# Linear attention into a routed feed-forward layer: every expert run twice, its first 256 rows after 16 routed tiles, the rest at the end

## The chip, the cores and the metric

One core of a Trainium2 chip. TensorE (PE) multiplies, VectorE (DVE), ScalarE (ACT) and GpSimd (POOL) work on tiles in SBUF and PSUM, SyncE (SP) issues transfers. The metric is the device time of one execution in microseconds; less is better. Inputs and outputs are in HBM, in 32-bit floats.

## The reference

```python
# attention: q, k, v of shape (8 batches, 8 heads, 576, 64)
kv  = einsum('bhsd,bhse->bhde', k, v)
out = einsum('bhsd,bhde->bhse', q, kv)
out = out / sqrt(mean(out*out, -1) + 1e-6) * g_norm
x   = out, heads side by side          # 4608 tokens x 512
# routed layer: 8 experts, each token goes to one
e_idx  = argmax(x @ w_gate)            # 512 x 8
gate_w = softmax(x @ w_gate)[e_idx]
eom    = sigmoid(x @ w_output_gate)
for e in range(8):
    rows = (e_idx == e)
    y[rows] = gate_w * eom[:, e] * (relu(x[rows] @ w1[e]) @ w2[e])   # 512 -> 1024 -> 512
```

How many tokens an expert gets is known only after the routing. The kernel gives the experts, sorted by their number of rows, fixed capacities (`CAP`: 704, 704, 640, 620, 600, 576, 576, 576 rows); what does not fit goes through an overflow loop at the end, which runs as often as a register says.

## The kernel before

Tokens are worked in 36 tiles of 128. **Attention**: `kv_part(b)` multiplies keys by values for one batch (4.5 tiles), `kvT_part` and `m_part` fold the gate weights in, and `out_tile(g)` multiplies a tile's queries by the result, so that one product gives the attention rows and the parts of the router's logits by head. ScalarE copies the rows (`xrow`), their squares (`sq`) and the logit parts (`gp`) out of PSUM; VectorE sums the squares (`sums`). Rows go to a table `xs` in HBM (`xwrite`).

**Routing** runs for a group of tiles at a time (`GR`: 10, 10, 4 and 12 tiles). `route(gi)` is a generator of some 40 small VectorE steps, with two groups of matmuls on TensorE (`rps`, which counts a token's place within its expert, and `tblps`, which sums the table of row numbers) and one-hot tiles `la` made mostly on GpSimd. `advance()` moves each routing to its next pause; where it is called is written out by hand (`WAITS`, `HOOKS`, `TAIL`).

**Experts**: a run of an expert takes up to 704 rows. `gather` fetches rows from `xs` by an indirect transfer on GpSimd's queue, `scale_rows` multiplies by the norm, `stage` transposes a tile on TensorE, and copies it as `xT`. For precision each operand is split into a high and a low part in a reduced format and each product is three matmuls: `split` makes `whi` (ScalarE) and `wlo` (VectorE, sometimes GpSimd) of a weight chunk of 512 KB that `wload` fetched on SP's queue; `mm1(i, f)` is an eighth of the first layer for all rows of run i, followed by the relu and the split of h (`hT`); `mm2(i, k)` is the second layer of one 128-row tile, followed by the scaling (`y`) and the indirect write to `out`. In a run's first layer the second-layer weights are split and the next run's first-layer weights loaded; in its second layer the next run's tiles are staged and its first-layer weights split, and its second-layer weights loaded.

**Order**: after 24 tiles the expert that leads by count so far is found on the chip (`lead_expert`), and its first 384 rows are run (`lead_run`) while the last 12 tiles are being routed. Then the rest of this expert and the seven others follow, in the order of their counts: `RUNS` has nine entries, and each weight is loaded and split once, 64 chunks of each kind. While the third run and the start of the fourth go on, `overflow_list` works out which rows did not fit and writes a small table (`tab`).

Within the blocks `with tc.manual_schedule(engines=...)` each engine works in the order in which the code issues; the engines meet by semaphores. Tiles in SBUF come from 30 slots of 4 KB a partition (`take`, `give`), in turn.

Of the kernel before, what the change touches and what calls it, by code (L numbers as in the profile page):

```python
# [21 lines left out]
P = 128  # L22
# [3 lines left out]
E = 8  # L26
# [10 lines left out]

CAP = [704, 704, 640, 620, 600, 576, 576, 576]  # L40
CMAX = max(CAP)
# [4 lines left out]
GR = (10, 10, 4, 12)  # L46
GROUPS = [list(range(sum(GR[:i]), sum(GR[:i+1]))) for i in range(len(GR))]
GMAX = max(GR)

LEAD_TILES = 24  # L50
LEAD_GROUP = [sum(GR[:i + 1]) for i in range(len(GR))].index(LEAD_TILES)
LEAD = LEAD_TILES * P // E // P * P

RUNS = [(0, 0, LEAD), (0, LEAD // P, CAP[0] - LEAD)] + [(p, 0, CAP[p]) for p in range(1, E)]


XD = min(4, 1024 // LEAD)
HF = 1024 // (2 * LEAD)

SLOTS = 30  # L60

SPARE = 3
# [3 lines left out]
BIG = {26: 5, 31: 5}  # L66

HOOKS = {15: 'R', 27: 'RR', 28: 'R', 31: 'RGW', 32: 'X', 34: 'NL'}
TAIL = "QLLLLRRRSLSRRSLLRRRLSLRRSRLSLL"

WAITS = {(0, 2): 3, (1, 7): 2, (1, 2): 0, (1, 8): 2, (1, 5): 0, (0, 8): 2, (0, 6): 2}

GPSIMD_GROUPS = 1
APART = (2,)


SPLITS = ['VV', 'AV', 'AV', 'AV', 'AP', 'AP', 'AP', 'AP']  # L80
NORMS = ("PPP", "VPVP")
PLACES = ['P', 'P', 'PAV', 'PAV', 'PAV']
# [14 lines left out]
K_I = K_C + E * TMAX  # L97
# [3 lines left out]
def constants():  # L101
# [13 lines left out]
    k[:, K_C:K_C + E * TMAX] = ((e[:, None] * NT + np.arange(TMAX)) * P).reshape(-1)  # L115
    k[:, K_I:K_I + P] = m
# [14 lines left out]
MAN = {ET.PE, ET.Activation, ET.DVE, ET.Pool}  # L131
# [3 lines left out]
def body(ctx: ExitStack, tc: tile.TileContext, kvm, rem, qT, wg, gn, w1, w2, kc, xs, tab, out):  # L135
# [3 lines left out]
    cst = ctx.enter_context(tc.tile_pool(name="cst", bufs=1))  # L139
    cf = cst.tile([P, K_N], F32, name="cf")  # L140
# [14 lines left out]
    gidx = cst.tile([P, E, TMAX], I32, name="gidx")  # L155
    oidx = cst.tile([P, E, TMAX], I32, name="oidx")
# [6 lines left out]
    ps_b = main.enter_context(tc.tile_pool(name="ps_b", bufs=2, space=psum))  # L163
    ps_t = main.enter_context(tc.tile_pool(name="ps_t", bufs=2, space=psum))
    ps_y = main.enter_context(tc.tile_pool(name="ps_y", bufs=1, space=psum))
    free = list(range(SLOTS))
    held = {}

    def take(shape, dt, name):

        i = free.pop(0)
        t = mem.tile(shape, dt, name=name, tag=f"slot{i}")
        held[id(t)] = (i, t)
        return t

    def give(t):
        free.append(held.pop(id(t))[0])
# [12 lines left out]
    def wload(p, which, c, eng=None):  # L190
        r = take([P, 1024], F32, "wraw")
        eng = eng or nc.sync
        src = (w1 if which == 1 else w2)[ds(expert(p, eng), 1), c]
        d = eng.dma_start(out=r, in_=src.rearrange("o p x -> p (o x)"))
        raw[(p, which, c)] = r
        return d

    def split(p, which, c, eng=None):
        r = raw.pop((p, which, c))
# [34 lines left out]
    def gather(i):  # L234
        p = RUNS[i][0]
        rows = xs[0:1 + LEAD_TILES * P] if i == 0 else xs
        for t, c0, M in tiles_of(i):
            x = take([P, XW], F32, "xg")
            nc.gpsimd.indirect_dma_start(  # L239
                out=x[:M, :], out_offset=None, in_=rows,  # L240
                in_offset=bass.IndirectOffsetOnAxis(ap=gidx[:M, p, t:t + 1], axis=0))
            xg[(p, t)] = x
# [6 lines left out]
    def scale_rows(i):  # L249
        for k, (t, c0, M) in enumerate(tiles_of(i)):  # L250
            if i < 2 and NORMS[i][k] == "V":
                continue
            scale_heads(xg[(RUNS[i][0], t)][:M], nc.gpsimd)

    def stage(i, k):
        p = RUNS[i][0]
        t, c0, M = tiles_of(i)[k]
        x = xg.pop((p, t))
        if i < 2 and NORMS[i][k] == "V":
            scale_heads(x[:M], nc.vector)  # L260
        if k == 0:
            if i == 0:
                xT[i] = [[take([P, XD, LEAD], F32R, "xT") for _ in range(4 // XD)] for _ in range(2)]
            else:
                xT[i] = [[mem.tile([P, 4, CMAX], F32R, name="xT", tag=f"xT{j}")] for j in range(2)]
        tl = cst.tile([P, 1], F32, name="tl", bufs=14)
        nc.vector.tensor_copy(tl[:M], x[:M, C_SCALE:C_SCALE + 1])
        tails[(p, t)] = tl
# [4 lines left out]
        for j, (hi, lo) in enumerate(zip(*xT[i])):  # L273
            n = hi.shape[1]
            v = ps[:, j * n:(j + 1) * n, :M]
            nc.scalar.copy(hi[:, :, c0:c0 + M], v)  # L276
            nc.vector.tensor_tensor(out=lo[:, :, c0:c0 + M], in0=v,  # L277
                                    in1=hi.bitcast(F32)[:, :, c0:c0 + M], op=ALU.subtract)
# [5 lines left out]
    def h_of(i, f):  # L284
        return hT[i][f // HF][:, f % HF] if i == 0 else hT[i][:, f]

    def mm1(i, f):
# [3 lines left out]
        J = 1 if C <= 512 else 2  # L291
        N = (C - T) // J
        hi, lo = ([a[:, d] for a in x for d in range(a.shape[1])] for x in xT[i])
        wh, wl = wgt[(1, f // 2)]
        if f == 0:
            if i == 0:
                hT[i] = []
            else:
                hT[i] = hp.tile([P, 8, 2 * CMAX], F32R, name="hT")
        if i == 0 and f % HF == 0:  # L300
            hT[i].append(take([P, HF, 2 * LEAD], F32R, "hT"))
        ps = ps_b.tile([P, 2, 512], F32, name="hps", tag="big")
        for d in range(4):
            o = d * 256 + (f % 2) * P
            for w, x, k in ((wh, hi, 0), (wh, lo, 1), (wl, hi, 2)):
                for j in range(J):
                    n = N + (T if j + 1 == J else 0)
                    nc.tensor.matmul(ps[:, j, :n], w[:, o:o + P], x[d][:, j * N:j * N + n],  # L308
                                     start=(d == 0 and k == 0), stop=(d == 3 and k == 2))
# [863 lines left out]
```

## Time and profile before

| | |
|---|---|
| median of 3 runs | 619.26 us (618.42 to 621.12) |
| the profiled execution | 620.81 us, span 618.8 us |
| TensorE matmul busy | 566.5 us, 92% |
| TensorE weight load busy | 506.3 us, 82% |
| VectorE, ScalarE, GpSimd busy | 263.2, 222.0 and 164.0 us |
| first expert matmul, last expert matmul | at 122.7 us, at 605.7 us |
| read from HBM, written | 72.6 MB, 20.0 MB |
| weight loads | 64 of 512 KB |

The span is counted from the first to the last instruction. A row of the timeline has the start, the duration, the engine, the line of the code and the operands; in brackets stands the idle time in front of it and what ended it. "L308" is the first layer's matmul, "L350" the second's, "L541" a tile's attention, "L474" keys by values, "L317" and "L318" the relu and the split of h, "L214" to "L224" the splits of weights. A matmul in full 32-bit floats (attention) shows as two records.

### The profile page before, as it was taken

The page shows a single profiled execution, that of the slowest core. Times are in us where ns is not written, and L with a number is a line of the kernel's source. Part 1 is how long each engine was busy: PE and PEld are TensorE (multiplying, and loading weights), DVE is VectorE, ACT ScalarE, POOL GpSimd, SP SyncE. Part 2 cuts the span into 40 slices and gives each one's busy share as a digit, 9 for nine tenths or more (in the row PEclk, how much of TensorE's full clock was granted, in tenths as well). Part 3 has the DMA queues.
Part 4 walks back from the last instruction along what each step waited for, and adds up shares of the span by engine and source line. Part 5 has one row for each costly group of instructions (what it writes and reads, how often), then busy time and mean ns, then how long its engine had stood idle before and what let it go on. Part 6 is the DMA issues. An engine that isn't in the chain of part 4 may idle for free.

```text
span 618.8 us, 10459 instructions
## 1 busy us (share of the span) xinstructions
PE 566.5 (92%) x4179; PEld 506.3 (82%) x4179; DVE 263.2 (43%) x536; ACT 222.0 (36%) x413; POOL 164.0 (27%) x163
## 2 busy tenths in 40 slices
PE   3799978848999999999899999999999999999991
PEld 3688868747898998889789988998799889889881
DVE  2123688699425456225331453235135325424300
ACT  1335545634225334323331343234234423523310
POOL 2001044443832510630036117104500630110010
PEclk9958777579999999999999999999999999999996
DMA  8999991770564622349776332524432451110010
GB/s 271 367 409 407 405 366 49 246 285 7 166 231 138 202 89 90 87 169 35 16 159 199 115 122 91 172 69 138 145 112 74 135 181 68 53 52 2 0 47 14
DMA packets 39122, 92.53 MB, mean 150 GB/s; under 512 B 14418, under 2 KB 14546, under 8 KB 39072
## 3 DMA queue, kind: packets, MB, share of 16 engines
q1 hardware_dynamic: 32176, 71.63, 37.4%
q0 software_dynamic: 6464, 20.00, 10.2%
q8 instruction: 34, 0.56, 0.4%
q10 hardware_dynamic: 432, 0.21, 0.1%
q14 instruction: 16, 0.13, 0.1%
HBM read 72.63 MB, written 19.99 MB: 150 GB/s over the span
## 4 chain that ended last, share of the span: by engine, by line
PE 57%; issue 19%; DMA 10%; DVE 4%; POOL 3%; ACT 3%; another core or an unknown queue 2%; SPq 0%; POOLq 0%; DVEq 0%
PE hps L308 24%; PE yps L350 23%; PE ops L541 3%; PE kvps L474 3%; DMA ld<-kvm 3%; DMA xs<-xrow 2%; PE tps L271 2%; POOL out L361 2%; DMA ld<-qT 2%; DMA ld<-rem 2%; PE yps L345 1%; POOL xg L239 1%; DMA wraw<-w 1%; DMA xg<-xs,gidx 1%
## 5 line engine op out<-in xcount | busy, mean ns | idle before, releaser
L308 PE MATMUL hps<-xT,whi 128*128 128x320 f32 (+4 forms) x1024 | 197.3, 310 | 9.5 <-DVE hT L318 8.4
L350 PE MATMUL yps<-whi,hT 128*128 128x512 f32 (+2 forms) x592 | 195.9, 399 | 1.0 <-ACT whi L221 1.0
L308 PEld LDWEIGHTS hps<-xT,whi 128*128 128x128 f32 x1024 | 163.6, 191 | 11.9 <-DVE hT L318 9.1
L350 PEld LDWEIGHTS yps<-whi,hT 128*128 128x128 f32 (+2 forms) x592 | 111.3, 188 | 25.2 <-ACT whi L221 1.2
L308 PE MATMUL hps<-xT,wlo 128*128 128x320 f32 (+4 forms) x512 | 121.6, 309 | 0.0
L318 DVE SCALAR_TENSOR_TENSOR hT<-hps,hT 128x512 fp32r<-128x512 f32 (+5 forms) x112 | 59.2, 529 | 142.6 <-ACT hT L317 142.3
L350 PE MATMUL yps<-wlo,hT 128*128 128x512 f32 (+2 forms) x296 | 116.6, 394 | 0.8 <-DVE wlo L224 0.8
L317 ACT ACTIVATE hT<-hps 128x512 fp32r<-128x512 f32 (+5 forms) x112 | 52.5, 469 | 164.0 <-PE hps L308 121.6
L308 PEld LDWEIGHTS hps<-xT,wlo 128*128 128x128 f32 x512 | 89.0, 191 | 0.0
L361 POOL DMA_INDIRECT out<-y,oidx x42 | 44.8, 1068 | 154.2 <-ACT y L360 107.2
L239 POOL DMA_INDIRECT xg<-xs,gidx x42 | 43.2, 1029 | 137.5 <-PE tps L271 54.6
L350 PEld LDWEIGHTS yps<-wlo,hT 128*128 128x128 f32 (+2 forms) x296 | 55.7, 188 | 12.1 <-DVE wlo L224 1.1
L217 DVE SCALAR_TENSOR_TENSOR wlo<-wraw,gcol,whi 128x1024 fp32r<-128x1024 f32 x32 | 43.9, 1372 | 39.6 <-ACT whi L214 39.6
L247 POOL TENSOR_TENSOR xg<-xg 128x512 f32<-128x512 f32 (+3 forms) x40 | 44.0, 1102 | 43.9 <-DMA xg<-xs,gidx 43.5
L541 PE MATMUL ops<-aug,ld 64*128 64x80 f32 (+1 forms) x640 | 49.0, 327 | 5.8 <-ACT gp L549 5.7
L541 PEld LDWEIGHTS ops<-aug,ld 64*128 64x128 f32 (+1 forms) x640 | 44.5, 230 | 8.8 <-ACT gp L549 6.4
L360 ACT ACTIVATE y<-yps,tl 128x512 f32<-128x512 f32 (+2 forms) x37 | 25.5, 689 | 71.4 <-PE yps L350 68.4
L276 ACT CAST xT<-tps 128x512 fp32r<-128x512 f32 (+3 forms) x45 | 23.6, 530 | 67.6 <-PE tps L271 63.9
L277 DVE TENSOR_TENSOR xT<-tps,xT 128x512 fp32r<-128x512 f32 (+3 forms) x45 | 27.7, 617 | 46.9 <-ACT xT L276 43.3
L474 PE MATMUL kvps<-ld 128*64 128x64 f32 (+1 forms) x640 | 36.4, 300 | 11.1 <-DMA ld<-kvm 10.7
L474 PEld LDWEIGHTS kvps<-ld 128*64 128x64 f32 (+1 forms) x640 | 33.1, 209 | 14.0 <-DMA ld<-kvm 12.0
L224 DVE TENSOR_TENSOR wlo<-wraw,whi 128x1024 fp32r<-128x1024 f32 x28 | 34.3, 1226 | 13.5 <-ACT whi L221 6.7
(158 smaller groups left out, 403.2 us busy)
## 6 DMA issues: line engine op xcount, KB each, us to landing
wraw<-w SPq DMA_DIRECT2D x64, 512.0 KB, 3.2
ld<-kvm SPq DMA_DIRECT2D x32, 512.0 KB, 10.2
ld<-qT SPq DMA_DIRECT2D x18, 512.0 KB, 10.2
xs<-xrow SPq DMA_DIRECT2D x13, 512.0 KB, 10.4
xs<-xrow SPq DMA_DIRECT2D x2, 1280.0 KB, 15.2
ld<-rem SPq DMA_DIRECT2D x3, 512.0 KB, 10.2
xg<-xs,gidx POOLq DMA_INDIRECT x42
out<-y,oidx POOLq DMA_INDIRECT x42
```

What stands on the lines that cost most here:

```text
L217: eng.scalar_tensor_tensor(out=lo, in0=r, scalar=gcol[:, 0:1], in1=hi.bitcast(F32), op0=ALU.mult, op1=ALU.subtract)
L224: eng.tensor_tensor(out=lo, in0=r, in1=hi.bitcast(F32), op=ALU.subtract)
L239: nc.gpsimd.indirect_dma_start(out=x[:M, :], out_offset=None, in_=rows, in_offset=bass.IndirectOffsetOnAxis(ap=gidx[:M, p, t:t + 1], axis=0))
L247: eng.tensor_tensor(out=v, in0=v, in1=f, op=ALU.mult)
L277: nc.vector.tensor_tensor(out=lo[:, :, c0:c0 + M], in0=v, in1=hi.bitcast(F32)[:, :, c0:c0 + M], op=ALU.subtract)
L308: nc.tensor.matmul(ps[:, j, :n], w[:, o:o + P], x[d][:, j * N:j * N + n], start=(d == 0 and k == 0), stop=(d == 3 and k == 2))
L317: nc.scalar.activation(hh, x, AF.Relu)
L318: nc.vector.scalar_tensor_tensor(out=v(h[:, l:l + n]), in0=x, scalar=0.0, in1=hh.bitcast(F32), op0=ALU.max, op1=ALU.subtract)
L350: nc.tensor.matmul(ps[:M], a, b, start=(f == 0 and k == 0), stop=(f == 7 and k == 2))
L361: i_ = nc.gpsimd.indirect_dma_start(out=out, out_offset=bass.IndirectOffsetOnAxis(ap=oidx[:M, p, t:t + 1], axis=0), in_=y[:M], in_offset=N ...
L474: nc.tensor.matmul(ps[u * D:(u + 1) * D, p * D:(p + 1) * D], k, v, start=(s == 0 and p == 0), stop=(s == 4 and p == NP - 1))
L541: nc.tensor.matmul(ps[r0:r0 + m, u, p * W:(p + 1) * W], qt[g // 2][r, p, q0:q0 + m], augs[b % 3][r, p, :], start=True, stop=True)
```

## The change

Every expert runs twice. Its first 256 rows (`ROWS_A`) run in the experts' natural order as soon as the first 16 tiles (`EARLY`) are routed; the rest, 448 to 320 rows of capacity, in the order of counts at the end. `RUNS` has 16 entries, and each weight is loaded and split twice. Where the first 16 tiles hold fewer than 256 rows of an expert, the rows of later tiles still begin at place 256 (`adj`).

The remaining 20 tiles are done by the generator `late()`: key/value products in three pieces, tiles one by one, then the routing's steps up to a pause. A piece follows each eighth of the first layer and each second-layer tile of the first seven runs, ten pieces a run. Their loads go on SP's queue between the weight loads, into eight slots of their own.

```diff
-GR = (10, 10, 4, 12)
+EARLY = 16
+TA = 2
+ROWS_A = TA * P
+GR = (8, 8, 10, 10)
-RUNS = [(0, 0, LEAD), (0, LEAD // P, CAP[0] - LEAD)] + [(p, 0, CAP[p]) for p in range(1, E)]
-SLOTS = 30
+RUNS = [(e, 0, ROWS_A) for e in range(E)] + [(p, TA, CAP[p] - ROWS_A) for p in range(E)]
+SLOTS = 22
+XSLOTS = 8
-GPSIMD_GROUPS = 1
-APART = (2,)
-SPLITS = ['VV', 'AV', 'AV', 'AV', 'AP', 'AP', 'AP', 'AP']
-PLACES = ['P', 'P', 'PAV', 'PAV', 'PAV']
+APART = (1, 2, 3)
+PLACES = ['P', 'PV', 'P', 'P']
+COLD = (2, 20, 8)
-MAN = {ET.PE, ET.Activation, ET.DVE, ET.Pool}
+MAN = {ET.PE, ET.Activation, ET.DVE, ET.Pool, ET.SP}
...
+    def constant(ps, n, start):
+        for _ in range(n):
+            nc.tensor.matmul(ps[0:D, 256:512], ones[:, 0:D], ones.unsqueeze(1).to_broadcast([P, 2, P]), start=start, stop=start)
...   in kv_part, which is now a generator of three pieces
+            if s < 4 and b < FIRST_B:
+                constant(ps, COLD[0] + (COLD[1] if b == 0 and s == 0 else 0), s == 0)
...   in out_tile
+                for c0 in range(r0, r0 + m, D):
+                    q0 = g % 2 * P + c0
+                    for u in range(2):
+                        r = slice(u * D, (u + 1) * D)
+                        nc.tensor.matmul(ps[c0:c0 + D, u, p * W:(p + 1) * W], qt[g // 2][r, p, q0:q0 + D],
+                                         augs[b % 3][r, p, :], start=True, stop=True)
-        nc.scalar.copy(gp[:, t].rearrange("q (p u) x -> q u p x", u=2), v[:, :, :, D:W])
+        nc.scalar.copy(gp[:, t].rearrange("q x (p u) -> q u p x", u=2), v[:, :, :, D:W])
...   at the end of route
+        tps = ps_t.tile([P, 2, E * TMAX], F32, name="tblps", tag="t")
+        for t in range(n):
+            nc.tensor.matmul(tps, las[t], rc[:, t, 0:2], start=(t == 0), stop=(t == n - 1))
+        yield from pause(9)
+        ... tacc gets or adds tps ...
+        if gi == EARLY_GROUP:
+            yield from rows_of_first()
+        if last:
+            yield from rows_of_all()
...
+    def early():
+        ... loads, key/value products of four batches and 16 tiles, with the first expert's first-layer weights behind ...
+        while squares:
+            sums()
+        load(late_loads, xfree, 2)
+        while routing:
+            advance()
+            if routing:
+                constant(ps_t.tile([P, 512], F32, name="cps", tag="t"), COLD[2], True)
+        for c in range(4):
+            wload(0, 2, c)
+        gather(0)
...
+    def run(i, unit):
+        for f in range(8):
+            mm1(i, f)
+            if f % 2:
+                split(i, 2, f // 2)
+                drop(1, f // 2)
+                if not last_run:
+                    wload(i + 1, 1, f // 2)
+            if f == 2 and not last_run:
+                gather(i + 1)
+            if f == 3 and not last_run:
+                scale_rows(i + 1)
+            unit(f)
+        ... staging, splits and loads for the next run between the second layer's tiles, as before ...
+        if i < E:
+            for k in range(T):
+                put(k, 3, unit, 8 + k)
...
+    rest = late()
+        split(0, 1, 0)
+        for k in range(TA):
+            stage(0, k)
+        split(0, 1, 1)
+        for i in range(E - 1):
+            run(i, lambda n: next(rest, None))
+    listing = overflow_list()
+        for i in range(E - 1, len(RUNS)):
+            run(i, lambda n: next(listing, None))
```

All 36 tiles use 64-row blocks of queries now, the splits are all ScalarE's and VectorE's, and the leading run with its search and its hand-written order is gone. In PSUM the late tiles have one pair of banks; the early ones have two.

More of the change, by code (lines that the diff above doesn't have):

```diff
@@ L154, in body @@
     slots = cst.tile([P, NT], F32, name="slots")
-    gidx = cst.tile([P, E, TMAX], I32, name="gidx")
-    oidx = cst.tile([P, E, TMAX], I32, name="oidx")
+    gidx = [cst.tile([P, E, TMAX], I32, name=f"gidx{w}") for w in range(2)]
+    oidx = [cst.tile([P, E, TMAX], I32, name=f"oidx{w}") for w in range(2)]
     novi = cst.tile([P, 1], I32, name="novi")
@@ L290, in mm1 @@
         T = half(i)
-        J = 1 if C <= 512 else 2
-        N = (C - T) // J
-        hi, lo = ([a[:, d] for a in x for d in range(a.shape[1])] for x in xT[i])
+        hi, lo = ([a[:, d] for d in range(4)] for a in xT[i])
         wh, wl = wgt[(1, f // 2)]
         if f == 0:
[L296 to L302, printed above, removed]
+            w = i // E
+            hT[i] = rp_[w].tile([P, 8, 2 * (ROWS_A, CMAX)[w]], F32R, name="hT", tag="hT")
+        ps = ps_h.tile([P, 512], F32, name="hps", tag="h")
         for d in range(4):
@@ L446, in body, with load @@
                 nq += 1
-    def load(spare):
+    late_loads = [l for l in loads if (l[1] >= EARLY // 2 if l[0] is qt else 2 * l[1] >= FIRST_B if l[0] is rt else l[1][0] >= FIRST_B)]
+    loads = [l for l in loads if not any(l is x for x in late_loads)]
+    def load(loads, free, spare=0):
         while loads and len(free) > spare:
@@ L495, in m_part @@
         a = augs[b % 3]
-        ps = ps_b.tile([P, 2, 512], F32, name="mps", tag="big")
+        ps = pair("mps")
         for i in range(2):
@@ L518, in out_tile @@
             gst[gi] = (sm.tile([P, GMAX, E], F32, name="ss"),
[L519 removed]
+                       sm.tile([P, GMAX, 16, H], F32, name="gp"),
                        sm.tile([P, GMAX, 16], F32, name="lg"))
         ss, gp, lg = gst[gi]
[L522 to L525 removed]
+        if not chunk:
+            chunk[:] = [g, take([P, 2, DM], F32, "xrow", xfree)]
         xrow = chunk[1][:, g - chunk[0]]
[L527 removed]
+        ps = pair("ops")
         parts = []
@@ L583, in pause @@
         def pause(k):
-            for _ in range(WAITS.get((gi, k), 1)):
-                yield 1
+            yield 1
         a = sm.tile([P, GMAX, E], F32, name="ra")[:, :n]
@@ L847, in p1_main, with late, more @@
             m_part(b, kvT)
-            while done_tiles < lim:
-                run_out(lim)
-        while done_tiles < NT:
-            run_out(NT)
-        for step in TAIL:
-            act(step)
+            more()
+            while run_out(lim):
+                more()
+        while run_out(EARLY):
+            more()
+        while squares:
+            sums()
+        load(late_loads, xfree, 2)
         while routing:
             advance()
+            if routing:
[3 more added lines that the diff above has]
+        gather(0)
+    def late():
+        def more():
+            load(late_loads, xfree, 1)
+        for b in range(FIRST_B, B + 1):
+            lim = tiles_ready(b - 1)
+            if b < B:
+                kv = kv_part(b)
+                for x in range(3):
+                    cp = next(kv)
+                    more()
+                    yield
+                    if run_out(lim):
+                        more()
+                        yield
+                kvT = kvT_part(cp)
+                yield
+                if run_out(lim):
+                    more()
+                    yield
+                m_part(b, kvT)
+                yield
+            while run_out(lim):
+                more()
+                yield
+        assert not late_loads and done_tiles == NT
+        while squares:
+            sums()
+            yield
+        while routing:
+            advance()
+            yield
     vec = nc.vector
@@ L945, in overflow_list @@
+        yield 1
+        gif = sm.tile([P, E, TMAX], F32, name="gif", bufs=1)
+        vec.tensor_reduce(out=gif[:, :, TA:], in_=t3, axis=AX.X, op=ALU.add)
+        yield 1
+        yield from places(1, gif, TA, TMAX)
     def overflow_list():
```

499 lines of the change are left out of this document (193 added, 306 removed).

## The prediction

> **What bounds the kernel now.** I read the page's slices first, then cut the span where the stages change, because the shares over the whole span mix stages with different limits. The columns are the stretch, its length, the busy time of PE, PEld, DVE, ACT and POOL, the granted clock, the DMA share and GB/s.
>
> ```profile
> core 0: us, PE busy (x) PEld busy (x) DVE busy (x) ACT busy (x) POOL busy (x), PEclk, DMA share, GB/s
> 0.00:34.70 34.70, 21.03 (x324) 17.97 (x324) 5.70 (x15) 7.80 (x19) 3.19 (x7) 0.91 0.95 329
> 34.70:56.00 21.30, 19.44 (x290) 17.84 (x292) 8.28 (x20) 11.29 (x30) 0.05 (x1) 0.66 1.03 408
> 56.00:122.70 66.70, 56.09 (x882) 51.15 (x880) 48.12 (x151) 35.70 (x97) 23.58 (x30) 0.70 0.78 277
> 122.70:158.70 36.00, 25.38 (x132) 22.97 (x132) 32.40 (x73) 13.86 (x26) 15.68 (x12) 0.84 0.44 152
> 158.70:606.00 447.30, 444.59 (x2555) 396.35 (x2555) 168.67 (x279) 153.00 (x242) 120.52 (x114) 1.00 0.39 108
> 606.00:618.80 12.80, 0.00 (x0) 0.00 (x0) 0.00 (x0) 0.39 (x1) 0.98 (x1) 0.59 0.03 11
> ```
>
> So there are 122.7 us of attention and routing before the first expert matmul, 36.0 us in which the leading run shares the chip with the last routing, 447.3 us in which TensorE stands still for 2.7 only, and a tail of 12.8. The sum is the span, 618.8. The dense stage is bound by TensorE at full clock; time can be won only in the first two stretches, and whatever goes into the dense stage on TensorE is paid in full.
>
> The second stretch is bad because of VectorE (32.40 of 36.0 busy). TensorE's rows, then VectorE's and GpSimd's:
>
> ```profile
> 122.74 1.15 PE L308 MATMUL hps<-xT,whi 128*128 128x384 f32 x2 [0.46 <-ACT xT L276]
> ...
> 137.04 1.01 PE L308 MATMUL hps<-xT,whi 128*128 128x384 f32 x2 [7.76 <-DVE hT L318]
> ```
>
> ```profile
> 129.38 0.26 DVE L605 SCALAR_TENSOR_TENSOR ry<-ru,ry 128x96 f32<-128x96 f32 x1
> 129.68 2.44 DVE L607 SCALAR_TENSOR_TENSOR ru<-ry 128x96 f32<-128x96 f32 x1
> ```
>
> ```profile
> 129.66 2.34 POOL L224 TENSOR_TENSOR wlo<-wraw,whi 128x1024 fp32r<-128x1024 f32 x1 [1.50 <-ACT whi L221]
> ```
>
> TensorE waits 7.76 us for a split of h that stands behind routing on VectorE, and one routing step takes 2.44 instead of 0.26 us while GpSimd splits a weight.
>
> **The expert work: unchanged on TensorE.** The 4996 capacity rows, 1536 first-layer matmuls and 42 tiles (5 of them halves) stay; only the cut differs (eight runs of 256 rows, then 448 to 320). Rates, from the chain:
>
> ```profile
> 174.85 14.27 PE hps L308 x96
> ...
> 447.42 25.60 PE hps L308 x192
> ...
> 477.61 0.44 PE tps L271 x4
> 478.05 5.48 PE yps L350 x24
> ```
>
> 320 columns cost 14.27/96 = 149 ns, and 288 on average (256 and 320 in turn) 25.60/192 = 133. The line through both gives 121 ns at 256, the average itself is the upper bound; over the 768 matmuls of the early runs that is between 0 and 9 us more. I take 121, since the 256s in that row already ran. A 256-row run is then 96 x 0.121 + 2 x (5.48 + 0.44) = 23.5 us. The whole dense work is 447.3 plus the leading run's 96 first-layer matmuls of 384 columns (by the same line 174 ns, 16.8 us): 464.1.
>
> **The first run starts earlier.** The loads keep their order, and the third key/value product ends with its last load as before:
>
> ```profile
> 34.73 1.00 PE L474 MATMUL kvps<-ld 64*64 64x64 f32 x13 [0.16 <-DMA ld<-rem]
> ```
>
> From 35.7 on, 11 of the 16 tiles remain, against 32 of 36 before. ScalarE paces them:
>
> ```profile
> L548 ACT ACTIVATE sq<-ops 128x512 f32<-128x512 f32 x36 | 21.9, 608 | 0.0
> L546 ACT COPY xrow<-ops 128x512 f32<-128x512 f32 x36 | 21.2, 590 | 21.5 <-PE ops L541 21.4
> ```
>
> ```profile
> 50.00:55.00 5.00, 3.97 (x68) 3.40 (x68) 3.64 (x11) 4.31 (x12) 0.00 (x0) 1.00 1.04 413
> 60.00:65.00 5.00, 3.56 (x90) 2.99 (x85) 4.02 (x5) 4.22 (x12) 0.00 (x0) 1.00 1.04 412
> 95.50:99.70 4.20, 4.20 (x76) 4.05 (x76) 4.10 (x16) 1.24 (x3) 4.20 (x8) 0.50 0.04 14
> ```
>
> 1.20 us plus a small third copy (I take 0.27) a tile, plus about 1 us for each of two batches, is 18.3 us; at ScalarE's 85% share of the first two rows 21.3. Tile 15 ends at 57.0. Two sums of squares follow (1.4). The added constant matmuls run in TensorE's waits and can only raise the clock; as ScalarE paces, I give them nothing. Then the routing of the last early group, which nothing covers. The last group of before took
>
> ```profile
> 125.83 2.39 DVE L589 TENSOR_SCALAR ra<-ss 128x96 f32<-128x96 f32 x1
> ...
> 155.30 0.28 DVE L940 CAST gidx<-gif 128x42 int32<-128x42 f32 x1
> ```
>
> 29.8 us for 12 tiles; without three steps lengthened by GpSimd (6), the splits between (7), a third of the size of the big steps (2) and the order of the experts (2) that is 12.5, to which 4 come back for the first group's rest: 16.5. That gives 75.0 for the row indices. From the gather to the first expert matmul:
>
> ```profile
> 110.86 1.08 POOL L239 DMA_INDIRECT xg<-xs,gidx  x1 [5.09 <-DVE oidx L900]
> ```
>
> 122.74 - 110.86 = 11.9 us with three tiles, 10 with two. The first matmul comes at **85**, 37.7 us earlier. Bounds: 80 with ScalarE full and nothing left of the first group; 98 if the routing takes the whole 29.8, or the four second-layer weight loads now issued just before the gather delay it.
>
> **What the late tiles cost.** 20 tiles and four key/value products move into the dense stage, on TensorE between the pieces of the first seven runs: no cover.
>
> ```profile
> 60.04 0.72 PE L541 MATMUL ops<-aug,ld 64*64 64x80 f32 x30
> ...
> 95.53 4.58 PE L474 MATMUL kvps<-ld 128*64 128x64 f32 x80
> ...
> 101.72 0.42 PE L489 MATMUL kvTps<-ident,kvc 128*128 128x128 f32 x2
> ```
>
> The new 64-row blocks have a row already (a tile across two batches, 32 parts, at full clock): 0.8 us, 16 for 20 tiles. The product took 4.58 at clock 0.50 (window row above); at full clock between 2.3 and 4.6, I take 2.7, nearer the half because TensorE was busy throughout: 10.8. Eight small groups of 0.42 and the two routings' counting matmuls (2.3 by rows of that length): 5.7. Together **32.5** (29 to 41).
>
> **Work doubled, but beside TensorE.** 64 more weight loads of 512 KB, 64 more splits. VectorE in seven early runs, by these rows:
>
> ```profile
> L217 DVE SCALAR_TENSOR_TENSOR wlo<-wraw,gcol,whi 128x1024 fp32r<-128x1024 f32 x32 | 43.9, 1372 | 39.6 <-ACT whi L214 39.6
> L224 DVE TENSOR_TENSOR wlo<-wraw,whi 128x1024 fp32r<-128x1024 f32 x28 | 34.3, 1226 | 13.5 <-ACT whi L221 6.7 <-DMA wraw<-w 5.9
> L562 DVE TENSOR_REDUCE ss<-sq 128x8 f32<-128x512 f32 x36 | 24.4, 680 | 13.5 <-ACT sq L548 13.5
> ```
>
> ```profile
> L318 DVE SCALAR_TENSOR_TENSOR hT<-hps,hT 128x256 fp32r<-128x256 f32 x8 | 3.4, 425 | 14.3 <-ACT hT L317 14.3
> ```
>
> A run: 4 x 1.37 + 4 x 1.23 + 8 x 0.43 + about 1.7 for the rows' split = 15.5; seven are 109, plus 13.6 for 20 sums and some 29 for two routings (two thirds of the 32.40 above is routing): 152 us against 7 x 23.5 + 32.5 = 197 on TensorE, 77%. ScalarE's sum is lower (some 136). DMA: 4.2 MB of weights, 1 MB of rows and about 4.4 MB of late traffic in 28 us, near 340 GB/s where 412 has been seen; a load has some 8 us until its split. So TensorE stays the bound, but VectorE in order has little slack, and TensorE is only two first-layer results ahead of it. SP's queue now carries late loads and row writes in front of weight loads, so a row write that waits for ScalarE holds a weight load. A late tile has one pair of PSUM banks instead of two: its three copies on ScalarE must end before the next tile's matmuls, while only one first-layer piece (12 x 0.121 = 1.45 us) lies between. Both are counted in the stalls. The splits that GpSimd made are gone; GpSimd keeps gathers, scatters and row scalings, 5 to 6 of 23.5 us a run. I take 14 us of stalls in seven runs (2 a run), and 5 at the start (a cold clock in the first results, splits not ahead). Below: 2.7 in 447 as in the dense row, so 3. Above: the third rival.
>
> The overflow list moves to later runs. Its table write was followed by
>
> ```profile
> 304.23 0.70 ACT L317 ACTIVATE hT<-hps 128x640 fp32r<-128x640 f32 x1 [5.69 <-remote]
> ```
>
> which cost TensorE, all told, at most the 2.7 us of idleness in the dense row and a slower clock for a moment. It now stands in the first of the longer runs, in front of one run's weight loads; I keep it at what it cost (0 to 6 us more, if ScalarE waits at a worse place). The removed choice of the largest expert, the extra correction of the counts and the contiguous reduction change VectorE by under 1 us each.
>
> **Sum**: 85 + 464.1 + 32.5 + 14 + 5 + 12.8 = 613.4 against 618.8. The profiled execution took 620.8, 2.0 over its span, and the median of the runs, 619.26, is 1.5 below it: **614**.
>
> **Rivals.** *Stalls absorbed*: the pieces fall where queues are free; stalls of 5 instead of 19 give 600. For it the 2.7 us of the dense row; against it VectorE's 38% there. *No earlier start to speak of*: the routing takes 29.8 or the gather waits; first matmul at 94 to 98, 622 to 627. For it that the chain is serial; against it that the splits are gone from it. *VectorE becomes the bound, slower than before*: in 56.00:122.70, with VectorE at 72%, TensorE was busy 56.09 of 66.7, 16% idle. The same idleness over the early runs makes 197 into 234, 23 more than my 211: 637; half of it gives 625. It decides from 5 us over my 14, 10% idle.
>
> The Trainium skill, SBUF — State Buffer, section Who interferes with whom, speaks for that rival: a VectorE instruction with two SBUF inputs and a GpSimd instruction that reads SBUF exclude each other for a whole instruction. The 2.44 beside the 2.34 above agrees. By it each of 14 row scalings on GpSimd (1.11 us by the row below) may hold up a weight split, 15.5 us of VectorE, taking it to 85%; all of it shown on TensorE, the sum would be 613.4 + 15.5 = 629. By the mean of the splits in this trace, which ran next to the same scalings, it is next to nothing, and the sum stays.
>
> ```profile
> L247 POOL TENSOR_TENSOR xg<-xg 128x512 f32<-128x512 f32 x34 | 37.7, 1112 | 37.9 <-DMA xg<-xs,gidx 37.6
> ```
>
> **Chances.** Mine 0.45 (own range 605 to 622), absorbed 0.2, no earlier start 0.1, VectorE the bound 0.25. What this kernel's runs can tell from no change is about 0.5%, 3 us: faster means under 616.2, so two thirds of mine and the absorbed case, 0.5; same (to 622.4) the rest of mine and some of the late start, 0.18; slower 0.32. The range leaves a tenth on each side: from under the absorbed case, 597, to most of the VectorE case, 635.
>
> **What would show it.** Right: first expert matmul near 85; PE near full from there with VectorE near 75% to about 300 us; late tiles' matmuls near 0.8 us each at clock 1.00. Wrong: waits of the first-layer matmuls for VectorE's h split or ScalarE's copies over 3 us a run; weight loads landing after their split is due; a first matmul after 95; first-layer matmuls of 256 columns above 125 ns.

## The result, and the profile after

The changed kernel takes 651.89 us (median of four, 648.93 to 660.41) where the kernel before took 618.84 beside it: a ratio of 1.051 (95% interval 1.046 to 1.057). It is slower by 5%, against a forecast of 614 and a range that ended at 635. One execution of the changed kernel, 660.41, was 1.8% slower than its fastest, and the ratio leaves it out. The profiled execution took 652.84 us with a span of 651.0.

Cut where the stages change, as before (stretch, length, busy time of PE, PEld, DVE, ACT, POOL, granted clock, DMA share, GB/s), the changed kernel shows:

```profile
core 0: us, PE busy (x) PEld busy (x) DVE busy (x) ACT busy (x) POOL busy (x), PEclk, DMA share, GB/s
...
61.40:80.60 19.20, 13.83 (x97) 10.51 (x96) 13.00 (x62) 0.47 (x2) 8.89 (x12) 0.73 0.51 173
80.60:96.20 15.60, 2.56 (x13) 1.52 (x10) 3.08 (x9) 1.23 (x3) 6.44 (x6) 0.63 0.78 275
96.20:232.30 136.10, 133.18 (x1655) 114.22 (x1656) 84.01 (x141) 83.35 (x156) 27.25 (x28) 0.98 0.74 260
232.30:293.10 60.80, 52.38 (x339) 45.83 (x338) 44.75 (x93) 27.36 (x42) 23.06 (x24) 0.97 0.63 197
293.10:317.00 23.90, 23.72 (x154) 21.40 (x154) 14.27 (x20) 13.55 (x20) 9.64 (x8) 1.00 0.67 210
317.00:346.70 29.70, 26.47 (x162) 23.48 (x161) 23.56 (x50) 14.52 (x22) 12.58 (x11) 0.94 0.54 173
346.70:404.70 58.00, 46.78 (x202) 39.07 (x201) 18.62 (x34) 16.95 (x24) 10.63 (x11) 0.88 0.94 112
```

The rows are: routing of the last early group; gather and first rows; runs 0 to 3; runs 4 and 5; run 6; run 7 (the last early one); run 8 (the first of the longer ones, 448 rows). Run 6 has neither late pieces nor the overflow listing, and takes 23.9 us with TensorE full: what a 256-row run costs when nothing disturbs it. In runs 9 to 15 little is amiss. The trouble stands in three places: 96.20 instead of 85 at the start; some wait or other in the early runs (runs 4 and 5 above all, 52.38 of 60.80 busy); and run 8, where TensorE is idle for 11 of 58 us at a clock of 0.88.

Run 8 first. SP's queue there, ScalarE's waits from 340 to 410, and the DMA engines from 346 to 400:

```profile
344.52 0.66 SPq L969 DMA_DIRECT2D tab<-met  x1
345.39 46.14 SPq L188 DMA_DIRECT2D wraw<-w  x7
```

```profile
ACT whi L208 <- DMA wraw<-w: 20.9, 2, 20.0
```

```profile
GB/s 274 250 39 23 16 22 47 47 29 36 29 29 39 23 23 10 10 13 6 12 3 12 12 12 49 24 30 46 103 46 367 331 325 413 416 422 401 146 167 237
DMA packets 7364, 6.13 MB, mean 113 GB/s; under 512 B 5888, under 2 KB 5888, under 8 KB 7361
```

The overflow table's write is `tab<-met`: 128 partitions by 44 elements, each 8 bytes from the next, so 5632 packets of 4 bytes. From the third slice of that row on (1.35 us each) the engines move 3 to 50 GB/s for 26 of them, some 35 us. The weight load right behind it on the same queue takes 42 us to land; the chain of waits in this stretch puts it as one piece:

```profile
345.39 42.32 DMA wraw<-w
...
387.79 1.16 ACT whi L208
```

Not only the transfers are late. SP's own instruction that issues this load took 29.5 us, where the median of the nine issues around it is 0.36 (shortest, median and longest in ns):

```profile
L188 SPq DMA_DIRECT2D wraw<-w x9: 333/360/29524, 341.4 to 391.2; - x9
```

So the loads behind it could go out only from 375 us on. TensorE itself stood still twice in run 8: 5.1 us for a gathered tile that came late, and 6.2 us for a transpose behind the late weight split.

At the start, the serial way from the routing to the first expert matmul (each row: start, length, engine, line, operation):

```profile
59.59 1.87 DVE L528 TENSOR_REDUCE ss<-sq 128x8 f32<-128x512 f32 x3
...
68.55 6.71 PE L411 MATMUL cps<-ones 128*64 128x256 bf16 x32
...
75.71 0.22 DVE L650 TENSOR_TENSOR rw<-rps,ohb 128x64 f32<-128x64 f32 x1 [3.11 <-PE rps L644]
...
80.05 1.96 SPq L188 DMA_DIRECT2D wraw<-w  x4
80.50 0.17 DVE L853 CAST gidx<-tbl 128x16 int32<-128x16 f32 x1
82.97 1.09 POOL L233 DMA_INDIRECT xg<-xs,gidx  x1 [3.32 <-issue]
89.91 0.69 DVE L241 TENSOR_TENSOR xg<-xg 128x512 f32<-128x512 f32 x1 [8.94 <-DMA xg<-xs,gidx]
96.20 1.31 PE L285 MATMUL hps<-xT,whi 128*128 128x256 f32 x2 [0.68 <-ACT xT L264]
```

And in the early runs, what TensorE waited for (from 96.2 to 350: in total, times, longest):

```profile
PE hps L285 <- DVE hT L290: 8.7, 8, 1.8
PE tblps L714 <- POOL la L686: 3.2, 7, 1.1
```

These are only the gaps ahead of an instruction; matmuls that follow a gap or a late piece also run longer. So I counted matmul by matmul: what a matmul took beyond its length in undisturbed runs (0.417 ns a column and 14 ns, a line through runs 6 and 9, 121 ns at 256 columns and 201 at 448) is a stall. Against the prediction's sum:

| term | predicted | measured | difference |
|---|---|---|---|
| first expert matmul | 85 | 96.2 | +11.2 |
| expert work at full rate | 464.1 | 459.8 | -4.3 |
| late work on TensorE | 32.5 | 30.8 | -1.7 |
| stalls, runs 0 to 6 (start included) | 19 | 26.1 | +7.1 |
| stalls, run 7 | 0 | 5.4 | +5.4 |
| stalls, run 8 | 0 | 16.9 | +16.9 |
| stalls, runs 9 to 15 | 0 | 2.8 | +2.8 |
| tail | 12.8 | 13.0 | +0.2 |
| span | 613.4 | 651.0 | +37.6 |

### The profile page after: what moved, and what is told of

It is laid out like the page before. It is cut to its first block, busy times and chain, and to the rows that moved or that the text cites. A ratio compares the mean times of both kernels' runs of the same rounds, so it can differ in the third digit from the quotient of the medians.

```text
span 651.0 us, 12185 instructions
## 1 busy us (share of the span) xinstructions
PE 575.8 (88%) x4825; PEld 498.1 (77%) x4825; DVE 338.1 (52%) x644; ACT 285.7 (44%) x481; POOL 169.6 (26%) x163
## 4 chain that ended last, share of the span: by engine, by line
PE 59%; issue 10%; DMA 8%; DVE 7%; POOL 4%; ACT 2%; POOLq 0%; SPq 0%; DVEq 0%; ACTq 0%
PE yps L316 26%; PE hps L285 24%; DMA wraw<-w 7%; PE tps L261 3%; POOL la L686 2%; DMA xg<-xs,gidx 2%; DVE wlo L218 2%; PE kvps L432 2%; PE ops L507 2%; PE yps L311 1%; ACT whi L215 1%; POOL out L328 1%; PE cps L411 1%; DVE ss L528 1%; DVE gp L577 1%
## 5 line engine op out<-in xcount | busy, mean ns | idle before, releaser
L285 PE MATMUL hps<-xT,whi 128*128 128x256 f32 (+5 forms) x1024 | 228.1, 314 | 10.2 <-DVE hT L290 9.3
L285 PE MATMUL hps<-xT,wlo 128*128 128x256 f32 (+5 forms) x512 | 158.6, 310 | 0.0
L290 DVE SCALAR_TENSOR_TENSOR hT<-hps,hT 128x256 fp32r<-128x256 f32 (+4 forms) x168 | 63.9, 400 | 109.3 <-ACT hT L288 102.1
L211 DVE SCALAR_TENSOR_TENSOR wlo<-wraw,gcol,whi 128x1024 fp32r<-128x1024 f32 x64 | 81.8, 1282 | 71.3 <-ACT whi L208 69.2
L288 ACT ACTIVATE hT<-hps 128x256 fp32r<-128x256 f32 (+5 forms) x128 | 55.9, 437 | 140.4 <-PE hps L285 136.1
L218 DVE TENSOR_TENSOR wlo<-wraw,whi 128x1024 fp32r<-128x1024 f32 x64 | 83.4, 1303 | 23.8 <-ACT whi L215 22.6
L208 ACT ACTIVATE whi<-wraw,gcol 128x1024 fp32r<-128x1024 f32 x64 | 73.3, 1150 | 20.9 <-DMA wraw<-w 20.9
L215 ACT CAST whi<-wraw 128x1024 fp32r<-128x1024 f32 x64 | 66.5, 1040 | 0.0
L261 PE MATMUL tps<-ident,xg 128*128 128x128 f32 (+3 forms) x168 | 26.3, 282 | 25.1 <-DVE tl L257 15.9
L686 POOL TENSOR_SCALAR la<-ni,rlon 128x128 bf16<-128x128 f32 x32 | 23.9, 763 | 83.2 <-DVE rlon L659 72.7
```

What stands on the lines that cost most here:

```text
L208: he.activation(hi, r, AF.Copy, scale=gcol[:, 0:1])
L211: eng.scalar_tensor_tensor(out=lo, in0=r, scalar=gcol[:, 0:1], in1=hi.bitcast(F32), op0=ALU.mult, op1=ALU.subtract)
L215: he.copy(hi, r)
L218: eng.tensor_tensor(out=lo, in0=r, in1=hi.bitcast(F32), op=ALU.subtract)
L261: nc.tensor.transpose(ps[:, c, :M], x[:M, c * P:(c + 1) * P], ident[:M, :M])
L285: nc.tensor.matmul(ps[:, :C], w[:, o:o + P], x[d][:, :C], start=(d == 0 and k == 0), stop=(d == 3 and k == 2))
```

## The experiments

The first four ran beside each other, then the next four, then the last four. Each group has its own runs of the kernel before (medians 620.18, 618.16, 619.99).

**The table's write.** One small copy ahead of it, so that a partition's 44 values are one piece:

```
-        nc.sync.dma_start(out=tab, in_=met[:, :, 0])
+        first = sm.tile([P, NOVER], F32, name="first")
+        vec.tensor_copy(first, met[:, :, 0])
+        nc.sync.dma_start(out=tab, in_=first)
```

> The changed kernel with the overflow table's first column copied into a tile of its own before it is written, so that each partition's row is one piece of 176 bytes instead of 44 pieces of 4 bytes. Theory: the 5632 small packets hold up the weight loads that stand behind them on SP's queue, and run 8 (the first of the longer ones), which lost 16.9 us to stalls and slow matmuls, falls to 2 to 4: 651.9 becomes 636 to 639. Rival: run 8 loses its time because eight weight loads and four gathers fall due at once there, whatever the table does: within 3 us of the changed kernel, with ScalarE still waiting over 10 us for a weight load around 370 to 390 us.

631.73 us, ratio 1.021 (1.016 to 1.025). Run 8 in its window, and the landing of the write and of the loads around it (issues, KB, median us):

```profile
342.10:383.60 41.50, 41.50 (x202) 35.53 (x201) 19.56 (x35) 17.13 (x24) 11.41 (x11) 1.00 0.47 154
```

```profile
wraw<-w SPq DMA_DIRECT2D x11, 512.0 KB, 3.6
...
tab<-first SPq DMA_DIRECT2D x1, 22.0 KB, 2.9
```

The theory holds, and by more than I gave it: run 8 falls from 58.0 to 41.5 us with TensorE full, the loads land in 3.6 us, and 1.051 becomes 1.021. The gain of some 19 us is over half of the 33 us that the change lost. 16.5 of it are run 8's. The profiled executions differ by another 4.7, at the start and in runs 1 to 7, which stand ahead of the write; those are no effect of it.

**The second-layer loads behind the first gather.**

```
+        gather(0)
+        mk = nc.gpsimd.memset(mark, 0.0)
         for c in range(4):
-            wload(0, 2, c)
-        gather(0)
+            d = wload(0, 2, c)
...   a dependency added by hand makes d wait for mk
```

> The changed kernel with the four second-layer weight loads of the first run issued behind the first gather (they wait for a mark on GpSimd behind it) instead of in front of it. Theory: the gather's rows, which took 5.9 us from the end of their issue to VectorE, queue behind 2 MB of weights; without them the first expert matmul moves from 96.2 to 91 to 93.5 and the time falls by 2.5 to 5 us. Rival: the 5.9 us is the gather's own latency and the first run then waits for its second-layer weights instead: first matmul at 95.5 to 96.5, time within 1.5 us or longer.

651.59 us, ratio 1.054 (1.048 to 1.059): no gain in time. The step itself did what was expected of it, for the first of two tiles:

```profile
84.75 1.09 POOL L233 DMA_INDIRECT xg<-xs,gidx  x1 [3.29 <-issue]
...
88.55 0.69 DVE L241 TENSOR_TENSOR xg<-xg 128x512 f32<-128x512 f32 x1 [5.77 <-DMA xg<-xs,gidx]
...
92.24 0.69 DVE L241 TENSOR_TENSOR xg<-xg 128x512 f32<-128x512 f32 x1 [0.48 <-DMA xg<-xs,gidx]
```

From the end of its issue the first tile's rows now come in 2.7 us instead of 5.9, so the 5.9 was a queue. The second tile's come 5.1 us after its own, now with the weights. From the gather's issue to the first expert matmul it is 10.0 us instead of 13.2, but in this execution the gather was issued 1.8 us later, as the last sums of squares ended 2.0 us later, and the first matmul stands at 94.8. Run 8 took 61.3 us here and 58.0 in the changed kernel's profiled execution, so a gain of this size can't be told in the time; it is taken up again below.

**No constant matmuls in the routing loop** (`COLD = (2, 20, 0)`).

> The changed kernel without the eight constant matmuls that TensorE runs at each step of the last early group's routing (those of the key/value products stay). Theory: the routing's counting matmuls stood 3.1 us behind 32 constant ones, and the table's matmuls some tenths more; without them the first expert matmul comes 3 to 3.5 us earlier and the time falls by as much. Rival: TensorE stands still for most of 20 us and is granted a lower clock for the first run, which gives the 3 us back: first matmul 92.5 to 93.5, but run 0 longer by 2 to 4 us and the time within 1.5 us.

652.84 us, ratio 1.056 (1.051 to 1.061), again nothing in the time. The counting matmuls come as soon as VectorE has their input, and VectorE's wait for them is gone:

```profile
71.77 0.42 PE L642 MATMUL rps<-ohb,ones 128*128 128x64 bf16 x8 [2.11 <-DVE ohb L607]
...
73.44 0.22 DVE L650 TENSOR_TENSOR rw<-rps,ohb 128x64 f32<-128x64 f32 x1
```

From the last sums of squares to the row indices it takes 15.9 us, against 19.0; the first matmul is at 93.5. Run 0 is not longer for it (34.7 us against 35.7), and its granted clock is 0.95 against 0.92, so the rival's lower clock is not seen: the constant matmuls kept no clock up that outlived the gather's wait.

**All late work in front of the first run**, in the same pieces, with nothing between the pieces of the early runs:

```
+        for _ in rest:
+            pass
         for i in range(E - 1):
-            run(i, lambda n: next(rest, None))
+            run(i, lambda n: None)
```

> The changed kernel with all of the late tiles' attention and routing run in front of the first expert run, in the same pieces, and nothing between the pieces of the early runs. Theory: it is the late pieces' VectorE and GpSimd work that makes the early runs wait; their 34 us of stalls and slow matmuls (runs 0 to 7) fall to 4 to 10, and the late work, now bare, puts the first expert matmul at 150 to 160: time 645 to 660. Rival: the early runs wait because their weights (4.2 MB and eight splits) come every 23.5 us instead of every 58: 25 us or more of stalls stay in runs 0 to 7, and the time is 668 to 680.

691.22 us. The part that decides between theory and rival is clear: runs 0 to 6 (first row below) take 169.3 us, and runs 1 to 6 (second row) 23.8 each, 0.4 over their matmuls.

```profile
182.90:352.20 169.30, 167.82 (x1066) 151.60 (x1067) 106.31 (x156) 96.20 (x141) 50.65 (x43) 0.99 0.68 214
...
209.30:352.20 142.90, 141.93 (x914) 128.24 (x913) 85.56 (x120) 81.25 (x120) 44.56 (x38) 1.00 0.70 220
```

So 4.2 MB of weights and eight splits every 23.8 us cost nothing here; the rival is out. The price for the late work was missed by 23 to 33 us, however: the first expert matmul came at 182.9, not 150 to 160, and the time lies above both forecasts.

```profile
96.00:182.90 86.90, 49.29 (x1071) 40.20 (x1068) 36.64 (x98) 31.61 (x77) 12.82 (x20) 0.60 0.58 192
```

Bare, in these pieces, no engine is busy more than 57% of that stretch and the clock is 0.60. Between the runs' matmuls the same work costs 49.9 us: 219.2 (row below, runs 0 to 6 of the version with the copied column that ran in the last group) less 169.3.

```profile
96.50:315.70 219.20, 209.48 (x2145) 182.29 (x2146) 143.49 (x254) 124.76 (x218) 58.79 (x59) 0.97 0.70 239
```

About 30 of it are its own matmuls, the other 20 are waits and longer matmuls around them.

**The start, three edits at once**, on the version with the copied column: the two above, and `PLACES[0] = 'PV'`.

> The changed kernel with the table's column copied (as in the first experiment, 631.7 us, first expert matmul at 94.8), and three edits to what stands ahead of the first expert matmul: no constant matmuls in the routing loop, the second-layer weight loads behind the first gather, and half of the first group's one-hot matrices on VectorE instead of all eight (5.92 us) on GpSimd. Theory: the 11 us by which the start was later than predicted are made of about 3 us of constant matmuls, about 3 of gather behind weights and the rest of rows that were squared later; the first expert matmul moves to 87 to 90 and the time falls by 4.5 to 7.5 us, to 624 to 627. Rival: the waits overlap, another step of the chain (the rows' write in front of the gather, the second gather) takes their place: first matmul at 92 to 95, time within 2.5 us of 631.7.

```profile
74.97 0.18 DVE L858 CAST gidx<-tbl 128x16 int32<-128x16 f32 x1
...
77.38 1.09 POOL L233 DMA_INDIRECT xg<-xs,gidx  x1 [3.34 <-issue]
...
80.98 0.69 DVE L241 TENSOR_TENSOR xg<-xg 128x512 f32<-128x512 f32 x1 [5.54 <-DMA xg<-xs,gidx]
```

The first expert matmul is at 87.0 us, as the theory said. The time is not: 629.43 us, executions from 626.9 to 633.1, ratio 1.020 (1.016 to 1.024) where the copied column alone had 1.021. That is inside the rival's 2.5 us. In the profiled execution (626.94) runs 1 to 3 took 102.0 us together, against 97.6 in the first experiment's, which gives back 4.4. The kernel with all edits, below, has 98.4 with the same start, and the third and fourth kernel of this group, without the three edits, have 100.8 and 101.0 on the same chip. So this looks like variation between executions or chips and not the edit; what sets it stays open.

**Row scalings on VectorE** (runs 1 to 8, at the end of the first layer, in place of GpSimd).

> The changed kernel with the table's column copied, and the row scalings of runs 1 to 8 on VectorE, at the end of the first layer, instead of on GpSimd. This adds 18 instructions of 0.69 us to VectorE. Theory: GpSimd's scalings hold up VectorE's instructions beside them (0.27 became 1.06, 1.22 became 1.93 in the run that prepares the four tiles of run 8), and TensorE waits for the h splits behind these; the 3.3 us of run 7 fall to under 1 and those of runs 3 to 5 (11.1) by 2 to 4; time 627 to 630. Rival: VectorE's in-order queue is the limit, whatever runs beside it; 12 us more work on it lengthens runs 3 to 5: 632 to 638. The Trainium skill, SBUF - State Buffer, section Who interferes with whom, speaks for the first.

646.47 us, ratio 1.046 (1.043 to 1.049): some 15 us worse, beyond the rival's figure. TensorE's waits for the h split fall, as the theory said (7.5 us in the first experiment, 3.3 here, from 130 to 350), but the transposes now wait for VectorE:

```profile
PE tps L261 <- issue: 6.8, 3, 3.3
PE tps L261 <- DVE xg L241: 5.5, 4, 2.5
...
PE hps L285 <- DVE hT L290: 3.3, 5, 1.0
```

The scaling waits for the gather in VectorE's order, and everything behind it there waits too. This is no clean test of what GpSimd does to VectorE; the last experiment is.

**One-hot matrices of the third and fourth group on VectorE.**

> The changed kernel with the table's column copied, and the one-hot matrices of the third and fourth routing group (20, 0.74 us each on GpSimd) built on VectorE at 0.24 us each. Theory: the 4.2 us in run 5 in which the table's matmuls wait for GpSimd go; VectorE's 4.8 us more come in pieces: time 627 to 629.5. Rival: VectorE is the bound in runs 4 and 5, so the wait moves to the first-layer matmuls (waiting for the h split): 631 to 635.

632.40 us. Run 5 is 27.0 us instead of 31.8, and TensorE waits for the one-hots 0.2 us instead of 3.2:

```profile
PE tblps L714 <- DVE la L686: 0.2, 1, 0.2
```

The place behaves as the theory said; VectorE has room there. The time lies in the rival's range all the same: the ratio, 1.024 (1.021 to 1.027), is no better than the base's 1.021 from another chip, with the longer runs 1 to 3 again. On one chip, below, the gain in run 5 shows.

**The listing from run 9 on.**

> The changed kernel with the table's column copied, and the listing of the overflow blocks from run 9 on instead of from run 7 on. Theory of VectorE's queue: the listing's steps between the h splits are what makes run 7 (28.0 us, 24.3 by its matmuls) wait: run 7 falls to about 25 and the time by 2.5 to 3.5 us. Rival: run 7 waits because GpSimd scales run 8's four tiles then, and VectorE's weight splits are held up with or without the listing: run 7 stays over 27 us, the time within 1 us of 631.7.

634.11 us, ratio 1.026 (1.023 to 1.030): no gain in the time, again with the longer runs 1 to 3. Run 7 in its window:

```profile
317.10:342.60 25.50, 24.80 (x162) 22.04 (x161) 15.93 (x24) 14.52 (x22) 12.38 (x11) 1.00 0.65 215
```

28.0 became 25.4 while GpSimd scaled the same four tiles. So the scalings alone don't make run 7 wait; the listing's steps have to stand there too.

**The kernel before with the same copy.**

> The kernel before with the table's first column copied into a tile of its own before it is written. In its trace the run that holds the write lost 4.7 us to late weight loads. Theory: these go, 614 to 616 against about 619. Rival: the loads behind the write were late without being waited for, and the 4.7 us are instruction fetches and splits that stay: within 1.5 us of the kernel before.

613.95 us against 619.99, ratio 0.989 (0.986 to 0.992): 6 us, a little more than its trace had suggested. The run that holds the write, before and with the copy:

```profile
270.60:333.20 62.60, 60.28 (x333) 53.81 (x333) 23.52 (x35) 19.54 (x26) 12.44 (x11) 0.97 0.75 103
```

```profile
269.70:327.40 57.70, 57.70 (x334) 52.61 (x333) 24.39 (x36) 19.64 (x26) 16.03 (x15) 1.00 0.38 126
```

**All that helped, together.**

> The changed kernel with all that helped: the table's column copied, no constant matmuls in the routing loop, the second-layer loads behind the first gather, half of the first group's one-hot matrices and all of the third and fourth group's on VectorE, and the overflow listing from run 9 on. Theory: the gains are in different places and add up. From the version with the start alone (629.4): 4.6 us in run 5, 2.2 in run 7, so 621 to 625. Rival: what is won at one place is waited for at the next, 627 or more. By either it stays above 618: the late work on TensorE (30 us) and what stalls are left (about 10) take what the earlier start (35.7) brings.

618.21 us (twelve runs) beside 633.24 for the copied column alone and 619.99 for the kernel before: a ratio of 0.998 (0.995 to 1.000). Here, on one chip, the gains show: 15 us. In the profiled executions, 631.8 less 618.0, they are 8.2 at the start (88.3 for 96.5), 5.5 in run 5, 2.5 in run 7, less 2.2 in run 10, where the listing now stands. It is better than forecast, but the kernel before with the copied column still beats it by 4 us. Runs 0 to 6:

```profile
88.30:301.50 213.20, 205.53 (x2145) 178.67 (x2146) 146.95 (x274) 124.62 (x218) 44.20 (x41) 0.99 0.73 250
```

In runs 0 to 6 TensorE is busy 205.53 of 213.20: what is left there is mostly the late work itself.

**The base again.**

> The changed kernel with the table's column copied, once more, as the base for the other kernels beside it: 630 to 635 by either theory.

633.24 us, ratio 1.020 (1.017 to 1.024), as the first time.

**Every scaling on GpSimd twice** in runs 1 to 8.

> The changed kernel with the table's column copied, and in runs 1 to 8 every row scaling on GpSimd done twice (the first time into a tile that nobody reads): 18 more GpSimd instructions of 1.1 us. Theory: a GpSimd instruction with two SBUF inputs holds up the VectorE instruction beside it, and VectorE's queue stands ahead of TensorE in these runs; 5 to 16 us longer than the base, the most in runs 3, 4 and 7, with waits for the h split. Rival: GpSimd is idle 70% of the time and VectorE's instructions seldom meet it: within 2 us of the base.

639.85 us beside 633.24: 6.6 longer, within the theory's interval, outside the rival's. Run 7 grows from 27.9 to 34.1 us, run 4 by 1.3, run 3 by 0.8, runs 1 and 2 not at all. GpSimd and VectorE in run 7, side by side:

```profile
322.61 1.97 POOL L241 TENSOR_TENSOR xg<-xg 128x512 f32<-128x512 f32 x1
325.11 1.04 POOL L249 TENSOR_TENSOR dbl<-xg 128x512 f32<-128x512 f32 x1 [0.53 <-DMA xg<-xs,gidx]
...
327.38 1.05 POOL L241 TENSOR_TENSOR xg<-xg 128x512 f32<-128x512 f32 x1
328.38 1.04 POOL L249 TENSOR_TENSOR dbl<-xg 128x512 f32<-128x512 f32 x1
329.50 1.91 POOL L241 TENSOR_TENSOR xg<-xg 128x512 f32<-128x512 f32 x1
```

```profile
323.60 1.06 DVE L920 TENSOR_TENSOR flew<-perm,cf 128x64 f32<-128x64 f32 x1
...
325.16 1.01 DVE L931 TENSOR_SCALAR cnp<-cnt 128x8 f32<-128x8 f32 x1
...
326.83 3.68 DVE L218 TENSOR_TENSOR wlo<-wraw,whi 128x1024 fp32r<-128x1024 f32 x1
330.44 1.00 DVE L936 CAST nov<-cei 128x8 f32<-128x8 int32 x1
```

A step on 64 elements a partition that takes 0.27 us by itself takes 1.06, one on 8 elements 1.01, a weight split 3.68 instead of 1.23. Each of the small ones ends within 0.1 us of the end of the GpSimd product beside it. The split waits for the products up to 329.42, ends 1.09 us later, which is about its own length, and holds up the next product in turn (1.91). Nine other weight splits of this execution start while a GpSimd product has over 0.25 us still to run, and all nine end 1.08 to 1.09 us after that product. The h split is not held up: 17 of 256 columns start beside a product in the same way and take 0.41 to 0.43 us, like the others. It only stands behind the held ones in the queue, and TensorE behind it.

## Why the prediction was wrong

**The largest miss is the overflow table's write.** The prediction said "I keep it at what it cost (0 to 6 us more, if ScalarE waits at a worse place)", and had noted that it would stand in front of one run's weight loads. The direction of the doubt was right and its size was not: run 8 lost 16.9 us, and the copy gives back 16.5 in that run. So the term of the sum that failed is the write's, put at nothing where 16.9 us were measured. The price had been read from the wrong view, TensorE's idle time. The views of the DMA engines in the kernel before (a window of 20 us, then the issues from 280 to 310 with their median time to landing) show what the write did where it stood:

```profile
284.00:304.00 20.00, 19.41 (x124) 18.35 (x123) 5.75 (x6) 4.69 (x6) 0.00 (x0) 1.00 1.10 7
```

```profile
wraw<-w SPq DMA_DIRECT2D x4, 512.0 KB, 26.6
```

The engines were full at 7 GB/s, and the loads behind the write landed after 26.6 us (the median of the two whose landing is on record). No split of these weights shows a wait in ScalarE's rows there, so they were still in time, and TensorE lost only 5 to 6. That loss goes back to ScalarE's waits of 4.24 and 5.69 us ahead of two relus, which the profile puts down to "remote", a release whose source it does not show; both are gone with the copy, and what they waited for stays open. In run 8 a load was due 22 us after its issue began (345.39 to 367.8), but landed after 42.3, and ScalarE waited for the 20 that lie between. The prediction counted what the write had cost TensorE, and not how long it held the queue: the issue of the load behind it took 14.0 us in the kernel before and 29.5 in run 8. Why the hold is longer here was not tried by itself; the trace shows that gathers and scatters share the engines with it, which in the kernel before they hardly did.

**The start** was given 85 us, with 80 to 98 as bounds; 96.2 is inside them and near the far one. Four things make up the 11.2, of which the runs moved two. The last sums of squares ended at 61.4, where the prediction's steps gave 58.4 (+3.0): ScalarE, which it took to pace the tiles at 85%, was busy 16.74 of the 26.70 us from 34.7 to 61.4 and waited 7.0 us for attention matmuls, so the last tile was copied by 60.1 and not by 57.0. The routing took 19.0 from there, not 16.5: the prediction gave the constant matmuls "nothing", as they "can only raise the clock", but 32 of them stood ahead of the counting matmuls; without them it was 15.9, so the estimate of the routing was right (its deductions leave 12.8 and not 12.5, a slip of 0.3) and the zero for the constants wrong (+2.5). From the row indices to the gather's start the sum had nothing, as the 10 us were counted from the gather; it took 2.5 (+2.5). In the four traces that have the landing of the last `xtail` write into `xs` (the first three experiments and the one with all that helped), the gather's wait ends 0.07 to 0.08 us after that landing, so it waits for this write and not for the indices alone. And from the gather to the first matmul it took 13.2, not 10 (+3.2): that is the four weight loads in front of the gather, which the prediction named as a reason for its upper bound and did not put in the sum; with the loads behind, it was 10.0. With the three edits the start is at 87.0 to 88.3.

**Late work and 256-row runs: right.** 30.8 us of late matmuls for 32.5, and a first layer of 256 rows in run 6 at 11.9 us for 96 matmuls, 124 ns on average against 121. (The line through the prediction's two rates gives 118 ns at 256 columns and 179 at 384, not 121 and 174; in its sum the slip is worth 2 us.) Of the 4.3 us by which the expert work came out below 464.1, 2.7 are idleness of the dense row that the prediction had left in. The doubled weight traffic beside TensorE costs nothing, as assumed (169.3 us for seven runs without late pieces).

**Stalls: the place right, the size short.** Runs 0 to 6 stalled 26 us where 14 and 5 were given. Its sign against, waits for the h split of "over 3 us a run", came only in run 7 (3.2 us; 2.6 in run 4, 1.7 in run 3, 1.0 in run 5). Runs 4 and 5 were idle 4.0 us each, for different reasons. Of run 5's, 3.2 was for GpSimd's one-hot matrices, which the prediction had left out ("GpSimd keeps gathers, scatters and row scalings"): building them elsewhere took 4.8 us off that run. Of run 4's, 2.6 was for the h split behind routing steps, the wait that it had named. Run 7, which it gave nothing, stalled 5.4, because the listing's steps meet the scalings of run 8's four tiles. Two more of its signs came: a first matmul after 95, and, in run 8, weight loads that landed after their split was due.

**The rivals.** *VectorE becomes the bound* told much of the story of runs 4 and 7, not the right price: runs 0 to 6 took 220.8 us, between my 216 (the start's 5 included) and its 234, and VectorE was busy 143 of them, 65%. It is an order and a meeting of two engines that cost, not a full engine. *No earlier start* was nearly right on the start (94 to 98), by its waiting gather and not by its long routing. No rival put the loss in run 8.

The Trainium skill, SBUF — State Buffer, section Who interferes with whom, was weighed in the prediction and set to nothing, since the mean of the splits showed nothing. The last experiment measures it: 18 more scalings cost 6.6 us, and run 7 alone grew by 6.2. By that page, a VectorE instruction with two SBUF inputs, and a cast or a tensor_scalar in one of its two-port modes, is shut out until a GpSimd instruction that reads SBUF and was there first has ended, while a tensor_reduce and an instruction with at most one SBUF input outside those modes are not. The trace agrees with it: 1.06, 1.01, 3.68 and 1.00 for the first kinds (in which mode the cast and the tensor_scalar ran it does not show), while the four sums of squares (a tensor_reduce) that start beside a GpSimd product take 0.67 to 0.68 as elsewhere, and the h split, one of whose two inputs is in PSUM, keeps its 0.41 to 0.43.

## What to carry to other kernels

When an operation moves, take its price from how long it holds its queue (its packets, a full DMA share at a low GB/s) and from when the work behind it is due, not from what it cost where it stood. A column of a small table is worth a copy before it is written; here that one line was 6 us in the kernel before and 19 in the changed one. Work that is put inside a TensorE-bound stage costs its own matmuls in full, and here about two thirds as much again in waits around them: 30 us became 50, which is more than the 36 us that the best start brought.

## What the runs showed of the hardware

A write of 22 KB in 5632 packets of 4 bytes holds the 16 DMA engines for 20 us or more with hardly another transfer beside it, and for some 35 when weight loads and gathers mix with it; SP's issue of the load behind it took 14.0 and 29.5 us, where 0.36 is usual. The same 22 KB in 128 packets lands in 2.9 us. The constant matmuls that keep TensorE busy ahead of a dependent chain are not free: 32 of them took 6.71 us, and the chain waited for 3.11 of it. And a VectorE step on 8 elements a partition can take 1 us instead of 0.17 when GpSimd is in the middle of an elementwise product.
